# Block-sparse attention and an exact-GELU feed-forward: the order of the value loads, the place of the first all-seeing values, and when the weights are asked for

## The chip, the cores and the metric

One core of one Trainium2 chip runs the kernel. The metric is device time in microseconds (us). Its engines work from queues of their own, each in order: TensorE (PE in the profile, PEld its weight loads), VectorE (DVE), ScalarE (ACT), GpSimd (POOL) and SyncE (SP). The loads from HBM that this text is about are asked for by GpSimd.

## The reference

Attention with a block mask, then a feed-forward without a residual. Blocks have 32 positions, so there are 24 of them.

```python
(batch, heads, seq, head_dim) = (4, 8, 768, 64)     # q, k, v, float32
scores = (1 / sqrt(64)) * q @ k.T
# block i sees block j if |i - j| <= 1, or i or j is the first or the last block,
# or j is one of three sampled blocks of i
scores = where(mask, scores, -1e9)
attn = exp(scores - max) / (sum + 1e-9)
x = (attn @ v)  # heads put side by side: 3072 tokens x 512
out = gelu_exact(x @ w_in) @ w_out     # w_in 512 x 2048, w_out 2048 x 512
```

## The kernel before

**Units.** Each batch is cut into two units of 384 tokens, so there are eight. A batch's first unit holds tokens of blocks 0 to 11, its second those of 12 to 23. The first unit also does the batch's two all-seeing ("dense") blocks, the first and the last, whose rows attend to all 24 blocks. A unit's other blocks go in groups of up to four. A round is the scores of two blocks of a group (`"s"`), or of one dense block for half of the heads (`"d"`). Unit 0 has four dense rounds (0 to 3) and six others (4 to 9): groups 0 (blocks 4 to 7), 1 (8 to 11) and 2 (1 to 3).

**Attention of a unit** (`attention`). Iteration `it` asks for, in this order: the scores of round it+1 on TensorE (into one of two banks), the division of what was weighed before, the transposition of round it-1, the maxima of round it+1 (VectorE), the exponentials of round it (ScalarE), the hooks of this iteration, `quota[it + 1]` steps of a filler on TensorE, a group's outputs (transposed on TensorE, copied by ScalarE), and then values that are due (`values`, a half at a time). `due` holds the iteration from which each half may go: the round that ends the group, plus one, plus one more for the second half. For unit 0 that gives 4, 5 for the dense values, then 6, 7, 8, 9, 10, 11; what is left at the end goes in a tail.

**Filler.** In the later units the filler is the second feed-forward product of the unit before. Unit 0 has none; there the filler is `idle_products`, products of an identity with queries whose result nobody reads.

**Feed-forward.** After its attention, a unit's first product and GELU follow (`ffn1_step`, L486 and L489, eight steps of two 128-wide parts), needing w_in; the second product (L508), needing w_out, fills the next unit's attention.

**Loads and gathers.** Values of block n lie in `kvs` in four groups of 32 partitions, two heads in each: heads 0 to 3 in groups 0 to 3, heads 4 to 7 in groups 1, 0, 3, 2. `load_v` (L133) loads one head, 32 partitions by 24 blocks by 64 elements, with a cast from float32 to bfloat16. `gather` (L277) copies the keys or the values of the three sampled blocks of each block, whose numbers are read from registers, into `gb`. In unit 0 the keys are gathered first (columns 0 to KC), and the values (KC to BW) by GpSimd from hooks at iterations 4, 6 and 8 (`values_of`), as the values land later. A hook's place sets the order within GpSimd's queue, not a time.

GpSimd's queue in unit 0, in order: loads of keys and queries of batch 0, eight value loads, w_in part 0, keys of group 1, w_in part 1, keys of group 2, w_in parts 2 and 3, values of group 0, w_out parts 0 and 1, values of group 1, w_out part 2, values of group 2, w_out part 3, keys and queries of batch 1 (six loads each), the gather for three blocks of unit 1; later, once SyncE's transposition of the queries has landed, the eight value loads of batch 1. Loads of GpSimd take eight semaphores in turn, so that each waits until the eighth before it has landed.

Of the kernel before, what the change touches and what calls it, by code (L numbers as in the profile page):

```python
# [19 lines left out]
def kernel(  # L20
# [10 lines left out]
    nc = tc.nc  # L31
    P = 128
    B, H, S, D = q.shape
# [10 lines left out]
    KC = NPR * BL  # L44
    BW = KC + 2 * V2
# [83 lines left out]
    def load_v(b, h):  # L129
        G, hh = divmod(h, 4)  # L130
        c0 = KC + V2 * G + VW * (hh % 2)
        hh ^= G
        nc.gpsimd.dma_start(out=kvs[b % 2][32 * hh:32 * hh + 32, 0:NB, c0:c0 + D],  # L133
                            in_=v[b, h].rearrange("(n p) d -> p n d", p=BL))

    def load_w_in(part, n=4):
        w = D_FF // n
        cols = slice(w * part, w * part + w)
        nc.gpsimd.dma_start(
            out=w_in_sb[:, :, cols], in_=moe_w_in[:, cols].rearrange("(ki p) f -> p ki f", p=P))  # L140

    def load_w_out(part, n=4):
        w = KOUT // n
        nc.gpsimd.dma_start(
            out=w_out_sb[:, w * part:w * part + w, :],
            in_=moe_w_out[P * w * part:P * w * (part + 1)].rearrange("(ko p) f -> p ko f", p=P))
# [28 lines left out]
    load_kq(qn, q, HALVES[0])  # L175
    load_kq(qn, q, HALVES[1])
    ones(0)
    for h in range(H):
        load_v(0, h)


    vf = const.tile([1, NB, NR], I32, name="vf")
# [89 lines left out]
    def gather(unit, js, at, c0=0, c1=BW, engine=None):  # L272

        src = k0 if (unit.b, c1) == (0, KC) else kvs[unit.b % 2][:, :, c0:c1]
        for j in js:
            for r in range(NR):
                (engine or nc.vector).tensor_copy(sampled(unit.place[j], r)[:, None, c0:c1],  # L277
                                                  src[:, bass.ds(at[j][r], 1), :])
# [235 lines left out]
    def idle_products(m):  # L514

        op = psO.tile([P, D_MODEL], F32, name="op")
        for _ in range(m):
            nc.tensor.matmul(op, lhsT=identity, rhs=qT0[:, 0].rearrange("p r s -> p (r s)"),
                             start=True, stop=True)
            yield  # L520
# [17 lines left out]
                                 start=(m == 0), stop=(m == KOUT - 1))  # L538
            store(n, quad, cols, op)

    def attention(unit, filler, quota, tail, hooks=None, late=False, ahead=None):

        done = begun.pop(unit, 0)
        rounds = [(unit, rnd) for rnd in unit.rounds[done:]]
        due = [(e - done + 1 + half, grp, half) for e, grp in sorted(unit.ends.items()) for half in range(2)]
        if ahead:
            begun[ahead] = AHEAD
            rounds += [(ahead, rnd) for rnd in ahead.rounds[0:AHEAD]]  # L550
        n, hooks = len(rounds), hooks or {}
        weighed, given = [], []

        def fill(m):
            for _ in range(m):
                next(filler, None)

        def weigh():
            _, grp, half = due.pop(0)
            values(unit, grp, half)  # L560
            if half:
                weighed.append(grp)

        def divide():
            divided(weighed[0])
            given.append(weighed.pop(0))
        for it in range(-1, n):
            last = it + 1 == n
            if not last:
                scores(*rounds[it + 1])  # L570
            else:
                while due and due[0][0] <= it:
                    weigh()
            ready = len(given)
            if weighed and not last:
                divide()
            if it >= 1:
                turned(rounds[it - 1][1])
            if weighed and last:
                divide()  # L580
            if not last:
                maxima(rounds[it + 1][1])
            if it >= 0:
                exponentials(rounds[it][1])
            store_finished()
            for f in hooks.get(it, ()):
                f()
            fill(quota[it + 1])
            if not late:
                store_finished()  # L590
            if ready:
                outputs(unit, given.pop(0))
            while not last and due and due[0][0] <= it:
                weigh()
        if not ahead:
            table(AF.Gelu)
        turned(rounds[n - 1][1])
        for f in hooks.get(n, ()):
            f()
        for m in tail[:-1]:  # L600
            fill(m)
            weigh()
        assert not due
        while len(given) > (not weighed):
            outputs(unit, given.pop(0))
        if weighed:
            divide()
        fill(tail[-1])
        outputs(unit, given.pop(0), 2)
        if ahead:  # L610
            table(AF.Gelu)
        for _ in filler:
            pass
        store_finished()
# [3 lines left out]
    grps = units[0].groups  # L618
# [14 lines left out]
    others = block_numbers(grps[1], POOL)  # L633
# [1 line left out]
    load_w_in(1)  # L635
    others |= block_numbers(grps[2], POOL)
    gather(units[0], grps[2], others, 0, KC, nc.gpsimd)
    load_w_in(2)
    others |= block_numbers(grps[0], POOL)
    load_w_in(3)  # L640

    def values_of(t):

        def ask():
            if t == 2:
                load_w_out(2)
            gather(units[0], grps[t], others, KC, BW, nc.gpsimd)
            if t == 0:
                load_w_out(0)
                load_w_out(1)  # L650
            if t == 2:
                load_w_out(3)
                load_by_token(kn, k, 1)
                load_by_token(qn, q, 1)
                others.update(block_numbers(J1[8:], POOL))
        return ask

    def more_numbers(js):
        def load():
            for c in range(0, len(js), 6):  # L660
                known.update(block_numbers(js[c:c + 6], DVE))
        return load
    attention(units[0], idle_products(33), [0, 3, 0, 4, 1, 3, 3, 2, 3, 3, 4], (3, 0, 4),
              hooks={0: [lambda: fixed(1)], 1: [lambda: fixed(2, nc.scalar.copy, 0)],
                     3: [lambda: fixed(2, nc.scalar.copy, 1)], 4: [values_of(0)],
                     6: [values_of(1)], 8: [values_of(2)], 10: [more_numbers(J1[:6])]})
# [5 lines left out]
    for n, unit in enumerate(units):  # L672
        nxt = units[n + 1] if n + 1 < len(units) else None
        b = unit.b
        fresh = nxt is not None and nxt.b != b
        if nxt is not None and not fresh:
            if n == 0:
                nc.vector.tensor_copy(kvs[0][:, :, 0:KC], k0)
                more_numbers(J1[6:8])()
            gather_fixed(keys(b), nxt.place)  # L680
            gather(nxt, J1[:8], known)
        for s in range(KOUT // 2):
            ffn1_step(n, 2 * s)
            if s == 0:
                if n == 0:
                    turn_keys()
                    turn_queries(1)
                    gather(nxt, J1[8:], others, engine=nc.gpsimd)
                    ones(1)
                    hold_loads(qT1[0:1, 0:1])  # L690
                    for h in range(H):
                        load_v(1, h)
                elif fresh and b + 2 < B:
                    xT, t0 = column[b, unit.groups[-2][0]]
                    hold_loads(xT[0:1, 0, t0:t0 + 1])
                    load_by_token(qn, q, b + 2)
                    load_by_token(kn, k, b + 2)
                    turn_queries(b + 2)
                elif nxt is not None and not fresh:
                    if b + 1 < B:  # L700
                        turn_keys()
                        hold_loads(g[0:1, 0, 0:1])
                        for h in range(H):
                            load_v(b + 1, h)
                    gather(nxt, J1[8:], others, engine=nc.gpsimd)
            if s == 7 and nxt is not None:
                table(AF.Exp)
                if n > 0 and not fresh and b + 1 < B:
                    next_keys(b + 1)
            if fresh and s == 0:  # L710
                gather_fixed(keys(b + 1), nxt.place)
                gather(nxt, J0[3:9], known)
                gather(nxt, J0[:3], known)
                hold_loads(sampled(nxt.place[J0[2]], NR - 1)[0:1, BW - 1:BW])
                gather(nxt, J0[9:], others, engine=nc.gpsimd)
        filler = ffn2_pieces(n)
        if nxt is None:
            last_output(n)
        elif fresh:
            attention(nxt, filler, [1, 7, 4, 3, 1, 5, 4, 7, 6], (2, 0, 6))  # L720
        elif b + 1 < B:
            attention(nxt, filler, [3, 11, 2, 5, 3, 8, 1, 7, 1], (5,), ahead=units[n + 2],
                      hooks={} if n else {
                          3: [lambda: next_keys(1)], 6: [more_numbers(J0[:3])]})
        else:
            attention(nxt, filler, [7, 6, 3, 5, 3, 8, 7], (1, 0, 5))
# [30 lines left out]
```

## Time and profile before

Three runs: 293.29, 294.49 and 298.87 us, median 294.49. The profile is of a fourth execution.

| what | us |
|---|---|
| time of the profiled execution | 296.14 |
| its span, first to last instruction | 294.4 |
| TensorE busy (share of the span) | 262.4 (89%) |
| VectorE, ScalarE, GpSimd busy | 213.5, 204.3, 118.8 |
| mean granted TensorE clock | 0.983 |
| batch 0: value loads asked for / landed | 6.32 to 13.00 / 14.17 to 25.37 |
| first feed-forward product of unit 0 | 45.61 |
| batch 1: value loads asked for / landed | 63.73 to 68.79 / 68.61 to 76.80 |

How to read it: times in the rows are from the start of the span. A busy share is a mean over stages with different limits, so the early stage is read by itself. In a timeline row come the start, the duration, engine, line, operation, output and inputs, the shape, how many instructions were merged, and in brackets the idle time of the engine ahead of it and what ended it. "issue" there means that the profile shows nothing that the engine waited for. In a row by stretches come busy time and instructions of PE, PEld, DVE, ACT and POOL, then the granted clock (1.00 is full), the DMA share and GB/s.

### The profile page before, as it was taken

What the parts mean: (1) busy time and instruction counts of PE and PEld (TensorE: products, weight loads), DVE (VectorE), ACT (ScalarE), POOL (GpSimd) and SP (SyncE); (2) the same over time, 40 slices, a digit from 0 to 9 for tenths busy, and PEclk for the clock granted to TensorE, in tenths of its full rate; (3) what the DMA queues carried; (4) which work ended last, traced back from release to release, by engine and by line L of the source; (5) the groups of instructions that cost most, each with busy time, mean ns of one, the idle gap of its engine ahead of it and who ended that gap; (6) DMA issues with size and microseconds to landing.
All of it is one profiled execution on the core that took longest, in us unless ns stands there. A gap on an engine that the chain in (4) does not pass through costs nothing.

```text
span 294.4 us, 11255 instructions
## 1 busy us (share of the span) xinstructions
PE 262.4 (89%) x4793; PEld 142.5 (48%) x4793; DVE 213.5 (73%) x477; ACT 204.3 (69%) x374; POOL 118.8 (40%) x219
## 2 busy tenths in 40 slices
PE   1667769978699999999999999999999999999994
PEld 1523445534354455635553555445544555355644
DVE  7595839989697887688997969688948878782000
ACT  8776645686267875698668975796778756976621
POOL 8697999734098000970495005920040014000000
PEclk9995999999799999999999999999999999999999
DMA  6999999999499711991199218991100210021001
GB/s 105 159 86 193 191 166 156 160 172 89 43 115 156 94 73 45 145 72 70 13 154 170 65 40 129 101 61 40 40 0 2 75 39 2 3 74 38 2 36 72
DMA packets 90628, 25.36 MB, mean 86 GB/s; under 512 B 81745, under 2 KB 87634, under 8 KB 90578
## 3 DMA queue, kind: packets, MB, share of 16 engines
q0 software_dynamic: 68352, 13.64, 86.7%
q1 hardware_dynamic: 22226, 11.01, 16.5%
q8 instruction: 37, 0.61, 0.8%
q14 instruction: 13, 0.11, 0.1%
HBM read 27.26 MB, written 6.29 MB: 114 GB/s over the span
## 4 chain that ended last, share of the span: by engine, by line
PE 55%; ACT 17%; DMA 9%; DVE 6%; POOL 6%; issue 4%; POOLq 0%; DVEq 0%; ACTq 0%
PE hp L486 22%; PE op L508 16%; PE av L436 9%; ACT pp L358 8%; DMA kv<-in_v_dram 4%; ACT L386 4%; POOL gb L277 3%; DMA qn<-in_q_dram 3%; ACT g L489 2%; PE sc L316 2%; DVE nm L341 2%; DMA kn<-in_k_dram 2%; PE tx L465 2%; PE av L537 2%; PE op L537 2%
## 5 line engine op out<-in xcount | busy, mean ns | idle before, releaser
L508 PE MATMUL op<-w_out_sb,g 128*128 128x512 bf16 x336 | 87.2, 385 | 0.1
L486 PE MATMUL hp<-xT,w_in_sb 128*128 128x384 bf16 x512 | 85.0, 326 | 0.8 <-ACT xT L473 0.4
L358 ACT ACTIVATE pp<-sc,nm 128x256 bf16<-128x256 f32 x176 | 75.4, 545 | 13.7 <-DVE nm L341 13.5
L489 ACT ACTIVATE g<-hp 128x768 bf16<-128x768 f32 (+1 forms) x72 | 52.1, 738 | 31.4 <-PE hp L486 31.4
L486 PEld LDWEIGHTS <-w_in_sb 128*128 128x128 bf16 x512 | 49.9, 98 | 36.1 <-issue 3.1
L341 DVE TENSOR_REDUCE nm<-sc 128x4 f32<-128x1024 f32 (+1 forms) x48 | 52.9, 1108 | 5.2 <-PE sc L316 5.1
L277 POOL COPY gb<-kv 128x388 bf16 (+1 forms) x87 | 36.9, 475 | 26.4 <-DVE gb L268 24.1
L508 PEld LDWEIGHTS <-g 128*128 128x128 bf16 x336 | 28.8, 98 | 35.4 <-issue 11.9
L277 DVE COPY gb<-kv 128x388 bf16 x177 | 44.2, 329 | 0.5 <-DMA qn<-in_q_dram 0.5
L436 PEld LDWEIGHTS <-pT 64*32 64x32 bf16 (+1 forms) x2400 | 26.3, 92 | 24.0 <-DVE pT L375 10.8
L375 DVE STREAM_TRANSPOSE pT<-pp 128x512 f32<-128x512 f32 (+1 forms) x48 | 31.5, 656 | 4.5 <-ACT pp L358 4.3
L436 PE MATMUL av<-kv,pT 64*32 64x130 bf16 (+1 forms) x1344 | 28.0, 220 | 7.4 <-issue 4.8
L473 ACT COPY xT<-tx 128x512 bf16<-128x512 bf16 (+1 forms) x32 | 13.6, 450 | 20.6 <-PE tx L465 20.6
L316 PE MATMUL sc<-gb,qT 64*32 64x256 bf16 x704 | 19.2, 277 | 8.5 <-ACT pp L358 4.5
L150 POOL COPY mark<-g 1x1 bf16<-1x1 bf16 x2 | 7.0, 3500 | 43.7 <-ACT g L489 43.7
L133 POOL DMA_DIRECT2D kv<-in_v_dram x32 | 22.9, 725 | 1.8 <-DMA qn<-in_q_dram 1.7
L316 PEld LDWEIGHTS <-qT 64*32 64x32 bf16 x832 | 11.6, 90 | 23.8 <-issue 18.0
L362 ACT ACTIVATE pp<-sc,nm 128x768 bf16<-128x768 f32 x16 | 17.1, 1101 | 6.5 <-DVE nm L344 6.5
L344 DVE TENSOR_REDUCE nm<-sc 128x1 f32<-128x768 f32 x16 | 15.0, 945 | 8.4 <-PE sc L316 7.9
L436 PE MATMUL av<-gb,pT 64*32 64x130 bf16 x1056 | 19.9, 222 | 0.0
L386 ACT ACT_TABLE_LOAD x15 | 19.2, 1283 | 0.3
L451 DVE TENSOR_SCALAR den<-av 128x8 f32<-128x8 f32 (+2 forms) x28 | 4.6, 164 | 20.3 <-PE av L436 18.7
(73 smaller groups left out, 244.5 us busy)
## 6 DMA issues: line engine op xcount, KB each, us to landing
out_dram<-os SPq DMA_DIRECT2D x23, 256.0 KB, 2.1
kv<-in_v_dram POOLq DMA_DIRECT2D x32, 96.0 KB, 7.0
kn<-in_k_dram POOLq DMA_DIRECT2D x18, 128.0 KB, 5.4
qn<-in_q_dram POOLq DMA_DIRECT2D x18, 128.0 KB, 5.2
w_in_sb<-in_moe_w_in_dram POOLq DMA_DIRECT2D x4, 512.0 KB, 11.1
w_out_sb<-in_moe_w_out_dram POOLq DMA_DIRECT2D x4, 512.0 KB, 7.9
kn<-in_k_dram POOLq DMA_DIRECT2D x2, 384.0 KB, 5.2
qn<-in_q_dram POOLq DMA_DIRECT2D x2, 384.0 KB, 7.2
```

Of the source, the lines that this page charges most:

```text
L133: nc.gpsimd.dma_start(out=kvs[b % 2][32 * hh:32 * hh + 32, 0:NB, c0:c0 + D], in_=v[b, h].rearrange("(n p) d -> p n d", p=BL))
L277: (engine or nc.vector).tensor_copy(sampled(unit.place[j], r)[:, None, c0:c1], src[:, bass.ds(at[j][r], 1), :])
L316: nc.tensor.matmul(o, lhsT=qT[rows, j // 4, pr, BL * (j % 4):BL * (j % 4) + BL], rhs=rhs(rows, pr), start=True, stop=True)
L341: nc.vector.tensor_reduce(out=nm[:, 0:2 * n].rearrange("p (g j) -> p g j", g=2), in_=A4[:, :, 0:n, :], op=ALU.max, axis=AX.X, negate=True)
L358: nc.scalar.activation(at[:, x // n, x % n], A[:, a:a + 256].rearrange("p (e c k) -> p e c k", e=2, k=BL), AF.Exp, bias=nm[:, x:x + 1])
L362: nc.scalar.activation(pp[:, 0:S].rearrange("p (c k e) -> p c e k", e=2, k=BL), A[:, 0:S].rearrange("p (c e k) -> p c e k", e=2, k=BL), AF ...
L375: nc.vector.transpose(pt.rearrange("p g c x -> p (g c) x")[:, :, 64 * s:64 * (s + n)].bitcast(F32), pp[:, 0:512 * n].bitcast(F32).rearrang ...
L386: nc.scalar.activation(junk, zero[0:1, 0:1], func)
L436: nc.tensor.matmul(av[32 * s:32 * (s + w), h, V2 * G:V2 * G + V2], lhsT=pv[rows, c % 4, BL * s:BL * (s + w), c // 4], rhs=src[rows], start ...
L486: nc.tensor.matmul(hp[:, i, 0:T], lhsT=w_in_sb[:, ki, (m + i) * P:(m + i + 1) * P], rhs=xTs[n % 2][:, ki, 0:T], start=(ki == 0), stop=(ki ...
L489: nc.scalar.activation(g[:, m + i[0]:m + i[1], 0:T], hp[:, i[0]:i[1], 0:T], AF.Gelu)
L508: nc.tensor.matmul(op, lhsT=g[:, m, t * P:(t + 1) * P], rhs=w_out_sb[:, m, :], start=(m == 0), stop=(m == KOUT - 1))
```

## The change

Three things change.

- All value loads of a batch go out in another order of heads: 0, 2, 1, 3, 5, 7, 4, 6. Their groups of partitions are then 0, 2, 1, 3, 0, 2, 1, 3, where they were 0, 1, 2, 3, 1, 0, 3, 2. So lower half (0 to 63) and upper half alternate.
- In unit 0, `when` sets the iterations of the values: 5, 6 for the dense halves, 7, 7 for group 0, then 8, 9, 10, 11 as before. The dense values stand behind the scores of one more round each. The idle products rise from 33 to 43: four more at it=2, two at it=3, four at it=4.
- w_in parts 2 and 3 are asked for behind the gather of group 0's values, w_out parts 0 and 1 behind that of group 1's, parts 2 and 3 behind that of group 2's. The order of the loads among themselves stays as it was.

```diff
+    VORDER = sorted(range(H), key=lambda h: (h // 4, (h % 4 ^ h // 4) % 2, h % 4))
+
+    def load_values(b):
+        for h in VORDER:
+            load_v(b, h)
...
-    for h in range(H):
-        load_v(0, h)
+    load_values(0)
...
-    def attention(unit, filler, quota, tail, hooks=None, late=False, ahead=None):
+    def attention(unit, filler, quota, tail, hooks=None, late=False, ahead=None, when=None):
...
         due = [(e - done + 1 + half, grp, half) for e, grp in sorted(unit.ends.items()) for half in range(2)]
+        if when:
+            due = [(at,) + x[1:] for at, x in zip(when, due, strict=True)]
...
     gather(units[0], grps[2], others, 0, KC, nc.gpsimd)
-    load_w_in(2)
     others |= block_numbers(grps[0], POOL)
-    load_w_in(3)
 
     def values_of(t):
 
         def ask():
+            gather(units[0], grps[t], others, KC, BW, nc.gpsimd)
+            for part in (2 * t, 2 * t + 1):
+                (load_w_in if t == 0 else load_w_out)((part + 2) % 4)
             if t == 2:
-                load_w_out(2)
-            gather(units[0], grps[t], others, KC, BW, nc.gpsimd)
-            if t == 0:
-                load_w_out(0)
-                load_w_out(1)
-            if t == 2:
-                load_w_out(3)
                 load_by_token(kn, k, 1)
                 load_by_token(qn, q, 1)
...
-    attention(units[0], idle_products(33), [0, 3, 0, 4, 1, 3, 3, 2, 3, 3, 4], (3, 0, 4),
+    attention(units[0], idle_products(43), [0, 3, 0, 8, 3, 7, 3, 2, 3, 3, 4], (3, 0, 4),
+              when=(5, 6, 7, 7, 8, 9, 10, 11),
```

The loops over the heads of the later batches become `load_values(1)` and `load_values(b + 1)` in the same way.

More of the change, by code (lines that the diff above doesn't have):

```diff
@@ L690 @@
                     hold_loads(qT1[0:1, 0:1])
-                    for h in range(H):
-                        load_v(1, h)
+                    load_values(1)
                 elif fresh and b + 2 < B:
@@ L702 @@
                         hold_loads(g[0:1, 0, 0:1])
-                        for h in range(H):
-                            load_v(b + 1, h)
+                        load_values(b + 1)
                     gather(nxt, J1[8:], others, engine=nc.gpsimd)
```

## The prediction

> **What bounds the kernel now.** I read the page's slices first, then the busy table by stretches, then the timeline of the first 84 us, then the landings of the value loads. From about 85 us on, the slices show TensorE at 9 tenths and over at full clock; nothing of the change works there except the order of later value loads. The time to win lies in the first unit and its neighbour.
>
> ```profile
> PE   1667769978699999999999999999999999999994
> PEclk9995999999799999999999999999999999999999
> DMA  6999999999499711991199218991100210021001
> ```
>
> Slice 3 (22 to 29 us) has the clock at 5 tenths, slice 10 at 7. The stretches of 3.41 us say why: TensorE was 1.69 us busy, or 1.07, in the stretch ahead of each slow one.
>
> ```profile
> 19.97:23.38 3.41, 1.69 (x36) 0.68 (x35) 3.41 (x6) 3.13 (x5) 3.29 (x11) 1.00 2.13 110
> 23.38:26.80 3.41, 1.83 (x49) 1.39 (x48) 1.68 (x2) 2.95 (x8) 1.51 (x5) 0.50 1.26 202
> 26.80:30.21 3.41, 3.41 (x75) 1.71 (x67) 1.22 (x1) 1.28 (x4) 3.41 (x10) 0.50 1.24 207
> 74.58:78.00 3.41, 1.07 (x72) 0.74 (x76) 1.28 (x2) 1.10 (x1) 0.00 (x0) 1.00 0.29 57
> 78.00:81.41 3.41, 3.41 (x53) 1.71 (x35) 2.61 (x7) 0.58 (x1) 1.01 (x2) 0.50 0.02 5
> ```
>
> The timeline (start, duration, and in brackets the idle time ahead with what ended it) shows the waits of unit 0 and, in the second fence, of unit 1:
>
> ```profile
> 22.04 1.58 POOL L139 DMA_DIRECT2D w_in_sb<-in_moe_w_in_dram  x2
> 25.51 1.47 PE L400 MATMUL av<-kv,ptd 64*64 64x130 bf16 x45 [1.58 <-DMA kv<-in_v_dram]
> 25.52 4.21 POOL L277 COPY gb<-kv 128x260 bf16 x12 [1.90 <-DMA kv<-in_v_dram]
> 26.91 0.63 PE L316 MATMUL sc<-gb,qT 64*32 64x256 bf16 x16
> 27.61 1.22 DVE L341 TENSOR_REDUCE nm<-sc 128x4 f32<-128x1024 f32 x1 [2.10 <-PE sc L316]
> 28.87 1.50 PE L400 MATMUL av<-kv,ptd 64*64 64x130 bf16 x48
> 37.88 0.37 PE L436 MATMUL av<-kv,pT 64*32 64x130 bf16 x24 [1.14 <-issue]
> 42.71 0.24 PE L436 MATMUL av<-kv,pT 64*32 64x130 bf16 x5 [1.34 <-issue]
> 45.61 10.56 PE L486 MATMUL hp<-xT,w_in_sb 128*128 128x384 bf16 x64 [0.41 <-ACT xT L473]
> ```
>
> ```profile
> 77.36 0.40 PE L436 MATMUL av<-kv,pT 64*32 64x130 bf16 x20 [2.34 <-issue]
> 79.42 2.23 PE L508 MATMUL op<-w_out_sb,g 128*128 128x512 bf16 x5
> ```
>
> Three things are to be seen. First, at 23.9 TensorE stands before the all-seeing values until the last value load has landed (25.37), and the scores queued behind it, free to go when exp 4 ends at 24.69, start 2.2 us late; VectorE's 2.10 us is that delay. Second, these products run at half clock: 1.50 us for 48, where the same 48 take 0.88 at 100.73. Third, the three stalls marked "issue" end 1.35 us after a 16 KB packet of the instruction queue has been read (packets end at 36.49, 41.39 and 76.00), and they lie about 256 instructions, or a multiple, apart: TensorE waits for its program. The packet is read 3.5, 2.6 and 4.4 us after TensorE entered the block before (about 32.0, 37.9, 70.6), while queue 0 is full; at 78.40, with the queue empty, after 1.04.
>
> **The value loads.** Each is 768 packets of 128 bytes into 32 partitions. Their heads fall into the lower (L) and upper (H) half of the partitions as L L H H L L H H; the change makes it L H L H L H L H. The eight land at 14.17, 16.26, 17.63, 19.11, 20.90, 22.12, 24.28 and 25.37. In the three later batches a load that follows one of the same half lands 1.50 us behind it (mean of 12: 0.91 to 2.26), one that follows a change of half 0.89 (mean of 9: 0.63 to 1.23). The first batch, queued ahead, speaks against this: 1.77 after a change, 1.47 without. Its packets, though, pass at 386 to 445 per us in some microseconds and at 734 to 829 in others, as if two halves served at once. So the last lands at 14.17 + 7 x 0.89 = 20.4 at one end, + 7 x 1.77 = 26.6 at the other. I take 20.4, as nine of twelve rows do; 1.13 us per load (22.1) would do as well, as GpSimd is not at the gather before.
>
> The Trainium skill (DMA: Bandwidth & Descriptors, "Rules for kernel authors") says of two transfers to disjoint halves "Don't bother — they serialize". By it the last load lands near 25 as now. The later batches disagree (0.89 against 1.50), the first agrees.
>
> **GpSimd.** Its keys end at 22.09. The two w_in requests that follow (2 x 0.74) move behind the gather of group 0's values, which starts at 22.1 and not 25.52. 12 copies of 0.346 = 4.2, two w requests 1.5, 12 copies 4.2, two requests 1.5, 9 copies 3.1, two requests 1.5: gathers end at 26.3, 32.0 and 36.6 (before: 29.7, 35.3, 39.2), the first key load is asked for at 38.1 (39.85). The order of DMAs is the same, so the eight semaphores that they share in turn (each request waits for the eighth before it) cost nothing new: w_out part 2, in front of the first query load, lands near 42 and that load is due at 43.4. w_in's last part lands near 34, is needed some 8 us after FFN1's start.
>
> **TensorE and VectorE, first unit.** Ten idle products more (128x512, 0.22 at full clock): four at it=2, two at it=3, four at it=4. They fill gaps of 1.37, 0.64 and the value wait (0.88, 0.44, 0.88), so cost nothing while the clock is full; the stretch 19.97 to 23.38 rises from 1.69 to some 2.7 busy, more than any stretch that was followed by a slow one, so I take full clock. At half clock they cost 0.43 each, 4.3 in all, of which the gaps cover about 3.
>
> Now forward. Scores 6 at 24.73 (ACT frees the bank at 24.69), three idle products, then dense half 0 at 25.8 to 26.7; scores 7 at 26.8, dense half 1 at 27.7 to 28.6; scores 8 at 28.6; the dense division 28.8 to 29.6, transpose 6, maxima 8 to 31.5. Group 0's two halves now stand together behind scores 8: 29.8 to 31.6, the division to 32.9, transpose 7 at 33.6. Before, that transpose ended at 36.4. Without stalls for instructions: group 1 at 33.7 to 35.4, division to 36.7, transpose 9 to 37.1, group 2 at 37.2 (its gather is done at 36.6) to 38.3, division and outputs as before (1.9 from the last value product to FFN1): 40.2.
>
> The stalls do not go for nothing, though. TensorE enters the block before the first of them at 28.7; by 3.4 + 0.95 + 1.35 the next is there at 34.4, 0.7 after group 1 could start. The one after comes 2.6 + 2.3 = 4.9 to 5.7 later, 39.3 to 40.1, take 39.8; group 2 goes on there, and before it went on at 42.71. So FFN1 starts at 42.7 and not 45.61: **2.9 us**. Ends: 0 (waits for the program longer by as much) and 5.4 (none). VectorE's chain to unit 1 (copy of the keys 1.80, fixed columns 3.8, gather 8.1, from 44.72 without a break to 58.37) starts with the last division and moves along.
>
> The Trainium skill (Runtime: NRT & Kernel Launch, "Instruction fetch mechanics") calls the crossing of a 16 KB block "mostly hidden". By that FFN1 starts at 40.2. This trace shows 1.14, 1.34 and 2.34 us.
>
> **Unit 1.** Batch 1's loads take 13.1 us from the first request (63.73) to the last landing (76.80), the program's packet is read only when they are through (75.01), and TensorE stalls 2.34; the idle stretch brings half clock at 78.0, where five products took 2.23 and not 1.08. At most 2.34 + 1.1 = 3.4 to win, at least 0. Requests come some 1.3 earlier, the burst ends some 2 us sooner; and 20 more instructions (ten weight loads, ten products) put the request ahead of a 1.30 us wait, and the need ahead of its place too. Half of the ends' distance: **1.7 us**.
>
> **Batches 2 and 3, and the rest:** 0; no stall over 0.6 us follows their loads, and those there wait for ScalarE's exponentials.
>
> **Sum.** 2.9 + 1.7 = 4.6. The profiled execution took 296.14 (span 294.4 and 1.7 around it): 291.5. It is 1.65 over the median of the runs shown, so by the median 294.49 - 4.6 = **289.9**.
>
> **Rivals**, all by the median.
> 1. The halves don't overlap, the loads end at 25.4 as now. Speaks for it: batch 0's own intervals. GpSimd then gathers at 25.5 to 29.7, 31.1 to 35.3, 36.8 to 39.9; dense values at 25.8 as above, group 1 from 35.4, group 2 at 40.0, FFN1 at 43.0. Unit 1 wins nothing. 294.49 - 2.6 = 291.9. Chance 0.2.
> 2. The program comes in time in both places (moved requests leave queue 0 free): 5.4 + 3.4 = 8.8, 285.7. For it: 1.04 at an empty queue. Against: the queue holds w loads from 28 to 44. Chance 0.2.
> 3. Slower: the moved w_in requests put their packets just where TensorE asks for its program. At half clock the block is entered at 31.0, and with the longest wait seen (4.4) twice, 31.0 + 6.7 + 6.7 = 44.4 against 42.71: 1.7 later, and unit 1's stall stays: 296.2. It decides, at half clock, once the two waits sum to over 42.71 - 31.0 - 4.6 = 7.1 (9.4 at full clock, with 28.7); now they sum to 6.1. Against: the queue is as full now. Chance 0.1.
>
> **How the numbers follow.** My forecast has 0.5. A measurement of this kernel can tell about 2%, 5.9 us, from no change. Faster by that (under 288.6): most of rival 2 and a fifth of the forecast, 0.28. Slower by over 2% (over 300.4) needs rival 3 three times over: 0.07. Within: 0.65. Range: from rival 2, 285.5, to rival 3, 296.2.
>
> **What would show it.** The last first-batch value load landing by 22; GpSimd's first value gather at 22.1; no wait on values at L400, and 0.9 per 48 products; the clock full through 30 us; L486's first product near 42.7; the stall near 72 to 75 shorter. Wrong: landing at 25 (rival 1), longer "issue" waits at L436 (rival 3), the half clock still there.

## The result, and the profile after

The changed kernel takes 291.84 us in the median of 12 runs (289.57 to 295.62), the kernel before 294.69 in 12 runs beside them. The ratio is 0.9852, 95% interval 0.9819 to 0.9885, so 4.4 us less (3.4 to 5.3); it is taken over the fast executions alone (five of the changed kernel's twelve, 294.2 to 295.6 us, are left out as slow), which is why it lies below the quotient of the medians. The profiled execution took 290.56 us, its span 288.7, against 296.14 and 294.4.

The page's slices of the kernel after. Slices 3 and 10 now stand at full clock (5 and 7 tenths before) and slice 4 shows 8 tenths; the DMA engines' slack of slice 10 (4 tenths before) is gone, and some lies in slice 3.

```profile
PE   1878479978998899979998999989988999899995
PEclk9999899999999999999999999999999999999999
DMA  6996999998999118991699119941001110011001
```

Busy time by stretches, columns as before (us, then busy PE, PEld, DVE, ACT, POOL, clock, DMA, GB/s):

```profile
19.97:23.38 3.41, 2.60 (x40) 1.18 (x41) 3.41 (x5) 3.13 (x7) 2.01 (x8) 1.00 1.26 204
23.38:26.80 3.42, 2.90 (x87) 1.32 (x85) 2.97 (x5) 3.04 (x8) 3.42 (x10) 1.00 0.54 91
26.80:30.21 3.41, 3.23 (x159) 2.05 (x160) 3.24 (x6) 2.73 (x7) 3.41 (x9) 1.00 0.73 100
30.39:33.80 3.41, 0.26 (x24) 0.16 (x9) 2.92 (x7) 1.71 (x4) 3.41 (x9) 0.99 1.27 204
33.80:37.20 3.40, 2.81 (x76) 1.56 (x84) 0.00 (x0) 1.27 (x4) 3.40 (x10) 0.50 1.12 161
```

The idle products fill 19.97 to 23.38 (2.60 us busy, 1.69 before), and the half clock of 23 to 30 us is gone. A new hole stands at 30.39 to 33.80, with TensorE busy for 0.26 us, and half clock follows it. The timeline of unit 0 after:

```profile
22.19 4.21 POOL L283 COPY gb<-kv 128x260 bf16 x12 [1.40 <-PE sc L322]
25.27 0.88 PE L406 MATMUL av<-kv,ptd 64*64 64x130 bf16 x48
26.96 0.88 PE L406 MATMUL av<-kv,ptd 64*64 64x130 bf16 x48
34.39 1.06 PE L524 MATMUL op<-qT,identity 128*128 128x512 bf16 x2 [3.74 <-issue]
41.30 0.34 PE L442 MATMUL av<-kv,pT 64*32 64x130 bf16 x14 [1.55 <-issue]
44.28 2.92 PE L492 MATMUL hp<-xT,w_in_sb 128*128 128x384 bf16 x17 [0.41 <-ACT xT L479]
45.44 0.88 POOL L111 DMA_DIRECT2D qn<-in_q_dram  x1 [2.17 <-DMA w_out_sb<-in_moe_w_out_dram]
```

Nothing waits for values any more; they landed at 21.29. The first feed-forward product (FFN1) of unit 0 starts 1.33 us earlier. TensorE waits longer than before where nothing is named (3.74 and 1.55), and GpSimd waits for w_out before it can ask for batch 1's queries. The timeline of unit 1 after:

```profile
48.00 4.70 POOL L111 DMA_DIRECT2D qn<-in_q_dram  x5 [1.68 <-DMA w_out_sb<-in_moe_w_out_dram]
67.59 5.64 POOL L133 DMA_DIRECT2D kv<-in_v_dram  x8
72.78 0.41 PE L442 MATMUL av<-kv,pT 64*32 64x130 bf16 x24
74.25 1.24 PE L514 MATMUL op<-w_out_sb,g 128*128 128x512 bf16 x5
76.07 6.15 PE L492 MATMUL hp<-xT,w_in_sb 128*128 128x384 bf16 x35
```

The 2.34 us stall is gone (24 products in one go at 72.78), the five products that took 2.23 us at half clock take 1.24, and FFN1 of unit 1 starts at 76.07 and not 82.23. From one unit's FFN1 to the next it is 31.79 us where it was 36.62: 4.83 of the 6.16 us won by then come from unit 1. From there to the span's end it is 212.6 us, 212.2 before. Batch 1's value loads are asked for 3.9 us later than before (67.59, 63.73) and take as long: 13.1 us from the first request to the last landing, both times.

### The profile page after: what moved, and what is told of

It is laid out like the page before. It is cut to its first block, busy times and chain, and to the rows that moved or that the text cites. A ratio compares the mean times of both kernels' runs of the same rounds, so it can differ in the third digit from the quotient of the medians.

```text
span 288.7 us, 11219 instructions
## 1 busy us (share of the span) xinstructions
PE 253.9 (88%) x4747; PEld 141.9 (49%) x4803; DVE 212.3 (74%) x477; ACT 204.6 (71%) x374; POOL 118.2 (41%) x219
## 2 busy tenths in 40 slices
DMA packets 90628, 25.36 MB, mean 88 GB/s; under 512 B 81745, under 2 KB 87634, under 8 KB 90578
## 4 chain that ended last, share of the span: by engine, by line
PE 52%; ACT 17%; DMA 11%; DVE 8%; POOL 6%; issue 4%; POOLq 0%; DVEq 0%; ACTq 0%
PE hp L492 20%; PE op L514 15%; PE av L442 9%; ACT pp L364 8%; ACT L392 4%; POOL gb L283 3%; DMA kv<-in_v_dram 3%; DMA kn<-in_k_dram 3%; DMA ptd<-kn 3%; DMA qn<-in_q_dram 3%; PE sc L322 3%; DVE nm L347 2%; DVE gb L283 2%; ACT g L495 2%; PE tx L471 2%
## 5 line engine op out<-in xcount | busy, mean ns | idle before, releaser
L514 PE MATMUL op<-w_out_sb,g 128*128 128x512 bf16 x288 | 75.9, 380 | 4.9 <-issue 3.9
L283 POOL COPY gb<-kv 128x388 bf16 (+1 forms) x87 | 37.0, 474 | 26.1 <-DVE gb L274 24.1
L283 DVE COPY gb<-kv 128x388 bf16 x177 | 43.6, 326 | 1.9 <-DMA qn<-in_q_dram 1.9
L133 POOL DMA_DIRECT2D kv<-in_v_dram x32 | 22.7, 721 | 1.1 <-DMA qn<-in_q_dram 1.0
L461 DVE TENSOR_TENSOR xh<-av,rec 128x512 bf16<-128x512 f32 (+2 forms) x28 | 18.3, 652 | 1.0
```

The lines of the kernel that those rows point to most:

```text
L461: nc.vector.tensor_tensor(xh[rows, :, 0:m * D].rearrange("p h (x d) -> p h x d", d=D), a[:, :, :, 0:D], rec[rows, :, 0:m, None].to_broadca ...
L514: nc.tensor.matmul(op, lhsT=g[:, m, t * P:(t + 1) * P], rhs=w_out_sb[:, m, :], start=(m == 0), stop=(m == KOUT - 1))
```

## The experiments

The result left four theories. **A:** unit 1 is faster because its value loads now start later, behind TensorE's request for its program. **B:** because alternating halves leave the DMA queue free sooner. **C:** because the ten idle products, twenty instructions, shift the request to an earlier place. **D**, for unit 0: the unnamed stalls are TensorE's program, which comes in packets of 16 KB, waiting behind weight loads.

The table has, from each run's trace: the landing of batch 0's last value load; FFN1 of unit 0; the first request for batch 1's values; the wait of the program's packet in unit 1, from TensorE's entry into the block before (counted in steps of 256 instructions) to the packet's start; the unnamed stall in unit 1; the time from unit 0's FFN1 to unit 1's; and the ratio to the kernel before with its interval.

| kernel | values landed | FFN1, unit 0 | batch 1's values asked for | packet's wait | stall | FFN1 to FFN1 | ratio |
|---|---|---|---|---|---|---|---|
| before | 25.37 | 45.61 | 63.73 | 4.3 | 2.34 | 36.62 | |
| after | 21.29 | 44.28 | 67.59 | 1.0 | 0 | 31.79 | 0.985 (0.982 to 0.989) |
| order_only | 22.24 | 43.63 | 60.24 | 4.8 | 2.96 | 36.40 | 0.988 (0.979 to 0.998) |
| when_only | 25.07 | 44.34 | 63.58 | 1.0 | 0 | 33.24 | 0.995 (0.990 to 1.000) |
| move_only | 25.02 | 46.31 | 69.41 | 1.5 | 0 | 31.25 | none |
| no_move | 22.74 | 46.33 | 62.56 | 4.4 | 2.38 | 35.94 | 1.003 (0.998 to 1.008) |
| late_loads | 24.14 | 44.56 | 67.61 | 1.0 | 0 | 32.18 | 0.988 (0.975 to 1.000) |
| no_order | 24.98 | 42.44 | 70.30 | 2.3 | 1.06 | 35.50 | 0.993 (0.984 to 1.001) |
| order_late | 22.58 | 43.73 | 66.22 | 1.2 | 0 | 31.74 | 0.986 (0.980 to 0.991) |
| weights_last | 21.81 | 39.26 | 71.76 | | | 42.31 | 1.005 (0.995 to 1.016) |
| w_out_later | 22.42 | 43.22 | 70.26 | 1.5 | 1.01 | 35.17 | 0.991 (0.987 to 0.995) |
| w_split | 21.98 | 40.70 | 69.69 | 2.4 | 2.15 | 36.66 | 0.991 (0.988 to 0.995) |

Each row is one profile. late_loads has the same unit 0 as the kernel before, and yet its values landed 1.2 us and its FFN1 started 1.05 us earlier: differences of a microsecond in one row are not read. In no_order, w_out_later and w_split the stall stands one block of 256 instructions earlier than in the other rows (it ends at 65.62, 66.37 and 64.98), so it belongs to the packet before the one in the column beside it; that one was read 2.8, 2.7 and 4.0 us after its request, while batch 1's keys were being transposed. For weights_last the request could not be placed; it has no unnamed stall of half a microsecond in unit 1.

**The parts one by one.** First the order of heads alone.

```diff
-    for h in range(H):
-        load_v(0, h)
+    load_values(0)        # and in the same way for the later batches; nothing else
```

> The kernel before with the new order of heads alone. Theory A (unit 1's 2.3 us stall goes because batch 1's value loads start later, at 67.6 and not 63.7, behind the request for TensorE's program): the first batch's last value load lands near 21.3, FFN1 of unit 0 starts 0.5 to 1.5 earlier (44.1 to 45.1), the value loads of batch 1 start at 62 to 64 as before and the stall at 75 stays; time 1 us less, ratio 0.995. Theory B (alternating halves leave the queue free sooner for the program): the stall goes here already; 4 to 5 us less, ratio 0.985.

The values landed 3 us earlier, FFN1 of unit 0 2 us. The stall of unit 1 stayed, 2.96 us, as A says and B does not. Its row of unit 1:

```profile
75.19 0.60 PE L442 MATMUL av<-kv,pT 64*32 64x130 bf16 x20 [2.96 <-issue]
```

Next the values' places and the idle products alone.

```diff
-    attention(units[0], idle_products(33), [0, 3, 0, 4, 1, 3, ...], (3, 0, 4),
+    attention(units[0], idle_products(43), [0, 3, 0, 8, 3, 7, ...], (3, 0, 4),
+              when=(5, 6, 7, 7, 8, 9, 10, 11),
```

> The kernel before with the values' new places and the ten idle products alone. Theory A: TensorE no longer waits for values (they land at 25.4, are needed near 25.3), full clock to 30 us, FFN1 at 44 to 45; batch 1's value loads start at 63 to 64, so unit 1's stall stays, 1 to 2.3 us: ratio 0.993. Theory C (twenty more instructions ahead move the boundary of the program's blocks, and so the request in front of the loads): the stall goes here: ratio 0.982 to 0.985.

Here TensorE found its values (0.88 us per 48 products at 25.24), and the time went into its program: three unnamed stalls of unit 0 of 1.94, 1.57 and 1.43 us, where the kernel before has 1.14 and 1.34. In unit 1 the stall was gone with loads at 63.58, as C says; the request came at 67.6, four microseconds into the loads, and was read within 1. A needs a bound, then: what matters is how deep in the loads the request falls. The ratio is A's (0.993 expected), though, and not C's.

Then the moved requests alone.

```diff
     gather(units[0], grps[2], others, 0, KC, nc.gpsimd)
-    load_w_in(2)
     others |= block_numbers(grps[0], POOL)
-    load_w_in(3)
...
+            gather(units[0], grps[t], others, KC, BW, nc.gpsimd)
+            for part in (2 * t, 2 * t + 1):
+                (load_w_in if t == 0 else load_w_out)((part + 2) % 4)
```

> The kernel before with the weight requests moved alone. Theory A: values still land near 25.4, the gathers and so the requests for batch 1's keys and queries come 1.5 later than before, wait for w_out's landings as well, and batch 1's value loads start at 67 or later: unit 1's stall goes, FFN1 of unit 0 is at 45 to 47; ratio 0.985 to 0.995. Theories B and C: the stall stays, the requests bring nothing or a loss of 1 us; ratio 1.00.

As A says: loads at 69.41, no stall, 31.25 us from FFN1 to FFN1, and a unit 0 that wins nothing (46.31). Its profiled execution took 292.41 us; there is no ratio for it.

**The whole change less one part.** Without the moved requests:

```diff
+    load_w_in(2)
     others |= block_numbers(grps[0], POOL)
+    load_w_in(3)     # and the requests of values_of(t) as in the kernel before
```

> The changed kernel with the weight requests where they were before. Theory A: batch 1's value loads start at 62 to 64, so unit 1's stall is back, 1 to 2.3 us; FFN1 of unit 0 at 43 to 44.5; ratio 0.990 to 0.993. Theories B and C: no stall in unit 1; ratio 0.980 to 0.985.

The stall is back with the early loads, twenty instructions or not, which leaves C alone with when_only. Unit 0 was worse than expected: unnamed stalls of 2.00 and 2.81 us, and half clock from 32 to 42 us behind them. Nothing of the gain is left. The timeline of unit 1:

```profile
76.19 2.08 PE L514 MATMUL op<-w_out_sb,g 128*128 128x512 bf16 x5 [2.38 <-issue]
```

Without the new order of heads (`VORDER = range(H)`):

> The changed kernel with the old order of heads. Theory A: values land near 25.1, the gathers end 3 us later than in the changed kernel, FFN1 of unit 0 at 44.5 to 46, batch 1's value loads at 69 to 70, no stall in unit 1; ratio 0.985 to 0.992. Theory B (the order is what frees the queue): first unit as before at 45.6 or worse and the stall back; ratio 0.995 to 1.00.

Values at 24.98 as expected, unit 0 better (42.44), its stalls only 0.64, 0.88 and 1.24; the packet for the second was asked for while queue 0 moved nothing (28.78 to 30.91) and was read after 1.1 us. GpSimd's queue ran 3 us later, so the turned keys of batch 1 landed at 65.9 (61.9 in the kernel after), VectorE waited for them, and TensorE for VectorE, 3.05 us at 66.0. A unit 1 without its old stall then won only 1.1.

Without `when` and the ten products:

> The changed kernel with the values' old places and the old number of idle products (order of heads and moved requests stay). Theory A: the first batch's values land near 21.5, FFN1 of unit 0 at 43.5 to 45, batch 1's value loads start at 67 to 68, no stall in unit 1; ratio 0.982 to 0.988, as good as the changed kernel. Theory C (the twenty instructions ahead are what unit 1 gains from): the stall is back, ratio 0.995.

This one decides nothing: there is no ratio for it, and its unit 1 is not compared. Up to unit 0's end it agrees with the others (values at 22.45, FFN1 at 43.9).

**The loads' time by itself.** The kernel before, with batch 1's value loads held until its keys are placed:

```diff
-                    hold_loads(qT1[0:1, 0:1])
-                    for h in range(H):
-                        load_v(1, h)
...
+    def late_values():
+        hold_loads(kvs[1][0:1, NB, 0:1])
+        for h in range(H):
+            load_v(1, h)
...
-                          3: [lambda: next_keys(1)], 6: ...
+                          3: [lambda: next_keys(1), late_values], 6: ...
```

> The kernel before with one thing changed: batch 1's value loads wait for that batch's placed keys (near 69) and not for its turned queries (63.5). Theory A (TensorE's program in unit 1 is late when its request, near 70, falls 6 us or more into the value loads): the loads start near 69, the packet of the program is read within 1.5 us of its request, the stall of 2.3 us and the half clock behind it go, FFN1 of unit 1 starts at 77.5 to 79 and not 82.2; ratio 0.985 to 0.99. Theory B (the order of heads or the first unit's other changes matter, not the loads' time): stall at 75 as before, ratio 1.00; a later landing (82 and not 77) may cost up to 1 us in unit 2.

```profile
67.61 5.66 POOL L133 DMA_DIRECT2D kv<-in_v_dram  x8
73.34 0.55 PE L436 MATMUL av<-kv,pT 64*32 64x130 bf16 x24
74.92 1.24 PE L508 MATMUL op<-w_out_sb,g 128*128 128x512 bf16 x5
```

Nothing but the start of eight loads moved, 3.9 us later, and unit 1 takes 32.18 us and not 36.62: the stall and the half clock go. That is A, with the bound that when_only set, shown by itself. FFN1 of unit 1 (76.74) was a little earlier than expected because unit 0 was.

Both effects, and nothing else of the change:

> The kernel before with the new order of heads and batch 1's value loads held for the placed keys, no other part of the change. Theory A: unit 0 as in order_only (FFN1 at 43.5 to 44.5, values landed near 22), no stall in unit 1 as in late_loads, FFN1 of unit 1 at 75 to 77; ratio 0.98 to 0.987, as good as the whole change or better. Theory C: the twenty instructions ahead are needed too, FFN1 of unit 1 at 79 to 80, ratio 0.99.

FFN1 of unit 1 at 75.47, ratio 0.986 (0.980 to 0.991): the order of heads and the later loads together give what the whole change gives. The two alone, 0.988 each, would make 0.976 if they added up; the intervals, up to 0.012 to each side, don't tell whether they do. Some of it goes again behind unit 1: from its FFN1 to the span's end it is 212.2 us before and 212.6 after, but 215.3 in late_loads, 215.9 in order_late and 215.4 in when_only. In unit 3 VectorE waits for batch 2's turned keys (4.71 us in late_loads, 2.77 before), and TensorE then for the exponentials (2.41 us in late_loads, 2.61 in order_late). With one profile of each it stays open whether this belongs to those kernels or to those executions.

**The program's packets in unit 0.** The changed kernel with the weights behind the last value gather:

```diff
             gather(units[0], grps[t], others, KC, BW, nc.gpsimd)
-            for part in (2 * t, 2 * t + 1):
-                (load_w_in if t == 0 else load_w_out)((part + 2) % 4)
             if t == 2:
+                for part in range(6):
+                    (load_w_in if part < 2 else load_w_out)((part + 2) % 4)
```

> The changed kernel with w_in parts 2 and 3 and all of w_out asked for behind the last value gather (near 33.7), so that queue 0 is empty from 26 to 35. Theory D (the 3.3 and 1.6 us stalls of unit 0 in the changed kernel are the program's packets waiting behind weight loads): the first goes, the second shrinks to under 1, FFN1 of unit 0 starts at 40.5 to 42 and not 44.3; batch 1's loads come 2 to 3 later, which may take back up to 2 us in unit 1; ratio 0.975 to 0.985. Rival (the stalls have another cause, such as the program's own order): both stay, FFN1 at 44; ratio 0.985 to 0.99.

```profile
31.77 0.59 PE L524 MATMUL op<-qT,identity 128*128 128x512 bf16 x2 [0.68 <-issue]
36.18 0.41 PE L442 MATMUL av<-kv,pT 64*32 64x130 bf16 x22
39.26 1.95 PE L492 MATMUL hp<-xT,w_in_sb 128*128 128x384 bf16 x11 [0.41 <-ACT xT L479]
...
60.15 0.41 PE L322 MATMUL sc<-gb,qT 64*32 64x256 bf16 x8 [2.34 <-POOL gb L283]
69.05 1.17 DVE L125 TENSOR_SCALAR kv<-ptd 128x768 bf16<-128x768 bf16 x4 [5.84 <-DMA ptd<-kn]
72.16 0.86 PE L442 MATMUL av<-kv,pT 64*128 64x130 bf16 x28 [4.76 <-DVE pT L381]
```

D is shown: with queue 0 empty (25.9 to 35.7) the packets start 0.9 and 1.1 us after their request and not 3.8 and 5.0, and 5.0 us of FFN1's start come back, more than expected. All of it is lost again in unit 1, and 5 us more: batch 1's keys land 6 us later behind the weights, VectorE waits 5.84 us for them and GpSimd's gather comes late too. The expectation allowed 2 us for that.

Three tries for a version that keeps both. In keys_first batch 1's keys stand ahead of w_out:

```diff
+            if t == 1:
+                load_w_in(2)
+                load_w_in(3)
             if t == 2:
                 load_by_token(kn, k, 1)
+                for part in range(4):
+                    load_w_out(part)
                 load_by_token(qn, q, 1)
```

> The changed kernel with the requests in another order: w_in parts 2 and 3 behind group 1's value gather, then group 2's gather, batch 1's keys, all of w_out, batch 1's queries. Theory D (the program's packets wait behind weight loads, and what weights_last won in unit 0 it lost because batch 1's keys came too late): FFN1 of unit 0 at 39 to 41 with at most one issue stall under 1 us; the keys land by 44 to 46 and not 53, the turned queries by 66, VectorE waits for neither; FFN1 of unit 1 at 72.5 to 75 (changed kernel: 76.1); ratio 0.97 to 0.98 to the kernel before. If w_out's last part lands after 53, the second product of unit 0 waits for it up to 2 us and half of that is gone. Rival (what unit 0 wins is always lost again to the queue's total load): FFN1 of unit 1 at 76 or later, ratio 0.985 to 1.00.

A ratio of 1.008 (0.998 to 1.019): a miss. Its one trace is read only for the order of the waits: FFN1 of unit 0 at 39.94 as hoped, the keys landed at 44.7, but their transposition, now beside w_out's packets, and w_out itself came late:

```profile
44.80 11.79 SPq L118 DMA_TRANSPOSE ptd<-kn  x1
57.52 0.59 PE L514 MATMUL op<-w_out_sb,g 128*128 128x512 bf16 x2 [1.83 <-DMA w_out_sb<-in_moe_w_out_dram]
```

In w_out_later all of w_out stands behind group 2's gather; in w_split, besides, w_in's last parts stand in the middle of group 1's:

```diff
+            gather(units[0], grps[t][:2], others, KC, BW, nc.gpsimd)      # w_split
+            if t == 1:                                                    # w_out_later: t == 0, behind the gather
+                load_w_in(2)
+                load_w_in(3)
+            gather(units[0], grps[t][2:], others, KC, BW, nc.gpsimd)
+            if t == 2:
+                for part in range(4):
+                    load_w_out(part)
```

> The changed kernel with all four w_out parts behind group 2's value gather (parts 0 and 1 were behind group 1's); w_in stays. Theory D: the first issue stall of unit 0 (3.3 us, its packet behind w_in) stays, the second (1.6 us, its packet behind w_out 5.0 us) shrinks to under 0.5, as queue 0 runs empty near 35; FFN1 of unit 0 at 42.5 to 43.5 and not 44.3; w_out's last part lands near 47.5 as now, so batch 1's queries are turned by 67 to 68 and unit 1 keeps the gain; FFN1 of unit 1 at 74 to 75.5 (changed kernel 76.1); ratio 0.978 to 0.985 to the kernel before. Rival (keys_first: unit 0's gain is lost to the queue again): FFN1 of unit 1 at 76 or later, ratio 0.985 to 0.99.

> As the run before it, with w_in parts 2 and 3 asked for 2 us later, in the middle of group 1's value gather, so that the program's packet asked for near 27.9 is read before they fill the queue. Theory D: first stall under 1 us, second under 1, FFN1 of unit 0 at 40.5 to 42; the turned queries at 67 to 68 then hold up unit 1's last rounds by 1 to 2 us; FFN1 of unit 1 at 73.5 to 75; ratio 0.975 to 0.983. Rival: queries later than 69, FFN1 of unit 1 at 76 or later, ratio 0.985 to 1.00.

Both met the expectation for FFN1 of unit 0 (43.22 and 40.70; w_split's second stall was 1.21, not under 1) and neither that of unit 1: the turned keys landed at 66.0 and 65.3, the first value product behind them waited for VectorE.

```profile
40.70 1.62 PE L492 MATMUL hp<-xT,w_in_sb 128*128 128x384 bf16 x9 [0.41 <-ACT xT L479]
65.36 1.17 DVE L125 TENSOR_SCALAR kv<-ptd 128x768 bf16<-128x768 bf16 x4 [4.53 <-DMA ptd<-kn]
68.47 0.86 PE L442 MATMUL av<-kv,pT 64*128 64x130 bf16 x28 [2.88 <-DVE pT L381]
```

That is w_split. The rival held: what unit 0 wins by an emptier queue, batch 1's keys lose. No version run here beats the changed kernel beyond the intervals; order_late equals it with less.

## Why the prediction was right, and where it was not

The predicted gain was 4.6 us, the measured one 4.4, and that they agree so well is luck. The two terms of the sum were wrong in opposite directions: 2.9 predicted for unit 0, 1.33 in the profile; 1.7 for unit 1, 4.83. The 1.33 is hardly more than the 1.05 us by which late_loads, with the same unit 0, differs from the kernel before.

**The value loads** (20.4; 21.29 measured). The alternating order works in batch 0: 21.3 to 22.7 in the seven runs with it that the table shows, 24.1 to 25.4 in the five without. The interval is 1.21 us in the kernel after and not 0.89; as the first load landed at 12.83 and not 14.17, the last still came before GpSimd's gather at 22.19. In batch 1 the 0.89 us per load did not come: 13.1 us for the eight, first request to last landing, before and after. Over the rows of the table it is 10.8 to 13.1 us with the order and 12.7 to 14.5 without, beside different traffic, so a gain there is neither shown nor excluded. The rule quoted from the Trainium skill (DMA: Bandwidth & Descriptors, "Rules for kernel authors"), that halves serialize, is contradicted by batch 0 (some 3 us of 25); batch 1 does not decide.

**GpSimd** was right to 0.1 us up to the keys: gathers from 22.19, ended at 26.34, 31.95 and 36.53, first key load at 37.99. Wrong was that the shared semaphores "cost nothing new": w_out part 2 landed at 45.16, not near 42, and the query loads waited 2.17 and 1.68 us.

**TensorE in unit 0.** Places and clock were right, half a microsecond early (dense halves at 25.27 and 26.96, 0.88 us each, full clock to 30). The entry into the block at 27.86 and its arrival at 34.01 agree with 28.7 and 34.4. The failed step is "the one after comes 2.6 + 2.3 later": its packet waited 5.0 us and not 2.6, behind w_out, so the block was there at 41.30 and not 39.8. That mis-sized wait is 1.5 of the 1.6 us missing. For no stalls the prediction gave 40.2; weights_last, with 0.68 us of stalls, reached 39.26.

**Unit 1.** The outcome was above the stated most of 3.4, and the mechanism was another: the burst did not end 2 us sooner but 3.9 later (80.73). The step that failed is "Requests come some 1.3 earlier". The first key request did (37.99, 39.85 before), but its packets did not. w_in part 2, now asked for behind the gather at 26.34, came too late to follow part 1, and queue 0 moved nothing from 25.36 to 27.79, where before it had no gap. What stands behind in it came 1.9 us later: w_out's last part (47.72, 45.84 before), batch 1's keys (53.25, 51.38) and so the start of their transposition. The queries' transposition follows on SyncE. Before, then after:

```profile
51.57 6.05 SPq L118 DMA_TRANSPOSE ptd<-kn  x1
57.90 3.67 SPq L121 DMA_TRANSPOSE qT<-qn  x1
53.44 6.35 SPq L118 DMA_TRANSPOSE ptd<-kn  x1
60.08 3.73 SPq L121 DMA_TRANSPOSE qT<-qn  x1
```

The turned queries landed 7.2 us behind their request and not 5.5 (why is not shown), at 67.30 and not 63.44, and the value loads wait for them. GpSimd's 2.17 and 1.68 us waits, which the prediction had set to nothing, are not what delayed this: the queries had landed at 58.63, ahead of the request at 60.08. So TensorE's request (67.7) came with the first value request (67.59), before any value packet ran, and its packet was read after 1.0 us. late_loads shows the effect of later loads alone. Of the 4.83 us, 2.34 are the stall, 0.99 the five products at half clock, 0.83 the values and transposes between the two, and 0.67 lies ahead of the stall, where VectorE's placing of the keys took 1.16 us with no value requests on GpSimd beside it and 1.61 with them (1.57 to 1.61 in the four rows with them, 1.16 or 1.17 in the others).

**The rivals.** Rival 1 (halves don't overlap) was wrong in batch 0. Rival 2 (the program in time in both places) came true in unit 1 only. Rival 3's mechanism, moved weight requests in front of the program, is what cost unit 0 its share, with a wait of 5.0 us beyond the 4.4 it assumed, without making the whole slower. Batches 2 and 3 gave 0 as predicted, within 0.5 us. (By rival 2's own sum the range should start at 285.7, not 285.5.)

## What to carry to other kernels

TensorE's program is a load too: here a packet of it for every 256 instructions, which waits while bulk loads are queued. Where a profile shows waits without a releaser at a fixed spacing in instructions, look when the packet of the instruction queue was read, and put bulk loads behind that request and not ahead of it. A request moved later can leave the queue empty, as between 25.36 and 27.79 here, and everything behind it comes later. An emptier queue at one place is paid for where the queue's last load is needed: follow that load before moving another.

## What the runs showed of the hardware that was not expected

- A 16 KB packet of the program started 0.9 to 1.1 us after its request when the software queue was empty (weights_last), and 2.6 to 5.0 us after it behind packets of 1 KB (unit 0, before and after); TensorE went on 1.3 to 1.5 us after the packet was read. Within eight value loads of 128-byte packets it was read after 1.0 to 1.5 us when asked for up to 4.0 us after the first request (after, move_only, late_loads, order_late, when_only), and after 4.3 to 4.8 us, with the loads nearly through, when asked for 6.6 to 7.7 us after it (before, order_only, no_move). The Trainium skill (Runtime: NRT & Kernel Launch, "Instruction fetch mechanics") has this cost "mostly hidden"; in the kernel before 34 of the 37 packets bring TensorE no unnamed stall over 0.4 us, and the other three cost 1.14, 1.34 and 2.34 us.
- The granted clock changes on a grid of 3.41 us. In the traces of all fourteen kernels, each full-clock stretch of that grid with TensorE busy for at most 1.50 us was followed by half clock (the 0.26 us at 30.39 to 33.80 in the kernel after among them), and each with 1.75 us or more by full clock; between 1.55 and 1.74 both occur.
- Transposing batch 1's keys took 6.05 us on SyncE in the kernel before, and 11.79 in the one trace of keys_first, where w_out's packets pass beside it. No other run tests whether w_out is the cause.
